# Decode attention on one core: w1 as the moving operand, and the last columns of the last K and V through transfers with an outermost dimension of three

## The chip, the cores and the metric

One core of a Trainium2 chip. The time is the device time of one execution in microseconds. In the profiles PE is the engine for matrix products (PEld its loading of weights), DVE the one for vectors, ACT for functions of single values, POOL is GpSimd, and SP only issues transfers here. Of the DMA queues, q1 carries the kernel's data (572.54 MB in before), q8 and q14 its instructions (40 packets and 14; the page calls both "instruction"). The landings and single packets given below (times of a semaphore's increments, lengths of packets) were read from the packed traces; the profile's views don't list them.

## The reference, cut to what matters

A gated mix of a one-token attention block (32 heads, a cache of 16384 positions of 128, batch 2) and an MLP block. The cache is 537 MB, the weights are 36 MB.

```python
def _A_ref(x, k_cache, v_cache, wq, wo):
    q = (x @ wq).reshape(B, Sq, H, Dh).transpose(0, 2, 1, 3)
    scores = jnp.einsum("bhqd,bhkd->bhqk", q, k_cache) * (Dh ** -0.5)
    p = softmax(scores, axis=-1)
    o = jnp.einsum("bhqk,bhkd->bhqd", p, v_cache)
    return o.transpose(0, 2, 1, 3).reshape(B, Sq, H * Dh) @ wo
# _B_ref: h = gelu(layernorm(x) @ w1) goes through shifts along the sequence;
# with one position every shift gives zeros, so x1 = x + 0 @ w2
# x1 + gelu(layernorm(x1) @ w3) @ w4;   result: g * a + (1 - g) * b
```

Softmax does not care in which order the positions stand, as long as K and V have the same order within a head.

## The kernel before

Two heads make one tile: 128 partitions, each with 256 consecutive positions (columns) of 128 bf16, 64 KB a partition. Three such buffers go round. All loads are issued on one queue (SP); `w4` and `wo` come last, `wo` in pieces that get smaller.

```python
    V_SPLIT_LAST = [NJ // 2, NJ // 2]          # NJ = 256
    def cache_rows(cache, i):
        b, hg = tiles[i]
        return cache[b, hg * G : (hg + 1) * G].rearrange("a s d -> (a s) d").rearrange(
            "(p j) d -> p j d", p=P)
    def load_k(i):
        t = big_tile("Kn")
        nc.sync.dma_start(
            out=t[:].rearrange("p (j d) -> p j d", d=Dh), in_=cache_rows(A_k_cache, i))
        kn_tiles[i] = t
    # ... load_v: the same, the last V in two pieces of 128 columns
    W4_SPLIT = [7] * 4
    WO_SPLIT = [4] * 6 + [2, 2, 1, 1, 1, 1]
    # ...
    def st_mix():                              # once, after the fifth V tile
        layernorm(xT[:], xn1T[:])
        h1 = const.tile([P, KC, B], FP32, name="h1")
        nc.vector.tensor_copy(out=h1[:], in_=linear("w1", xn1T)[:])   # w1 stationary: 64 matmuls
        gelu(h1[:], hT[:], KC)
        # ... x1 = xT + linear("w2", zeros); layernorm(x1); start_out
```

Of the kernel before, what the change touches and what calls it, by code (L numbers as in the profile page):

```python
# [10 lines left out]
FP32 = mybir.dt.float32  # L11
BF16 = mybir.dt.bfloat16
ACTF = mybir.ActivationFunctionType
ALU = mybir.AluOpType
# [9 lines left out]
def kernel(  # L24
# [15 lines left out]
    nc = tc.nc  # L40
    P = nc.NUM_PARTITIONS
    B, Sq, D = A_x.shape
    _, H, Sk, Dh = A_k_cache.shape
    F = B_w3.shape[1]
    assert Sq == 1 and Dh == P and B == 2 and H == 32
    G = 2
    NJ = G * Sk // P
# [4 lines left out]
    KC = D // P  # L52
    FC = F // P
    scale = float(Dh) ** -0.5
    NHG = H // G
    NT = B * NHG
# [5 lines left out]
    const = ctx.enter_context(tc.tile_pool(name="const", bufs=1))  # L62
# [8 lines left out]
    def misc_psum(shape, dtype=FP32):  # L71
        return mps.tile(shape, dtype, tag="misc", name="misc")

    def big_tile(name):
        return big.tile([P, SLOT], BF16, tag="big", name=name)

    def t_tile(shape, dtype, name="T"):
        return tpool.tile(shape, dtype, tag="T", name=name)
# [4 lines left out]
    kn_tiles = {}  # L83
    vn_tiles = {}
    wt = {}
    V_SPLIT_LAST = [NJ // 2, NJ // 2]

    def cache_rows(cache, i):
        b, hg = tiles[i]
        return cache[b, hg * G : (hg + 1) * G].rearrange("a s d -> (a s) d").rearrange(  # L90
            "(p j) d -> p j d", p=P
        )

    def load_k(i):
        t = big_tile("Kn")
        nc.sync.dma_start(
            out=t[:].rearrange("p (j d) -> p j d", d=Dh), in_=cache_rows(A_k_cache, i)
        )
        kn_tiles[i] = t

    def load_v(i):
        t = big_tile("Vn")
        tv = t[:].rearrange("p (j d) -> p j d", d=Dh)
        src = cache_rows(A_v_cache, i)
        j0 = 0
        for n in V_SPLIT_LAST if i == NT - 1 else [NJ]:
            nc.sync.dma_start(out=tv[:, j0 : j0 + n, :], in_=src[:, j0 : j0 + n, :])
            j0 += n
        vn_tiles[i] = t

    def load_rows(keys, srcs):

# [26 lines left out]
    def load_first():  # L139
# [12 lines left out]
        out=perm[:].rearrange("k (h a) -> k h a", a=4),  # L152
        in_=ident_f[:].rearrange("k (a h) -> k h a", a=4),
# [26 lines left out]
    for g in range(1, 4):  # L180
        nc.vector.tensor_tensor(
            out=osel_f, in0=osel_f, in1=ident_f[:, 40 * g : 40 * g + 8], op=ALU.add
# [9 lines left out]
        out=pick[:], in_=ident_f[:].rearrange("p (g w) -> p g w", w=32)[:, :, 0:B]  # L192
# [28 lines left out]
    omg_bc = const.tile([P, B], FP32)  # L221
# [21 lines left out]
    def group(g):  # L243
        return slice(32 * g, 32 * g + B)

    def zero_rows(ps, g, width):
        nc.tensor.matmul(
            ps[32 * g : 32 * g + 32, :],
            lhsT=perm[:, 0:32],
            rhs=zero[:].to_broadcast([P, width]),  # L250
            start=True,
            stop=False,
            skip_group_check=True,
        )
# [180 lines left out]
    def start_out(x1):  # L435
        for g in range(NQ):
            zero_rows(out_acc, g, QW)
        res = const.tile([P, KC, B], FP32, name="cen")
        nc.vector.tensor_tensor(out=res[:], in0=x1, in1=over_r(omg_bc[:]), op=ALU.mult)
        for c in range(KC):  # L440
            for g in range(NQ):
                nc.tensor.matmul(
                    out_acc[group(g), c:QW:KC],
                    lhsT=res[:, c, :],
                    rhs=ident_f[:, 32 * g : 32 * g + 32],
                    start=False,
                    stop=False,
                    skip_group_check=True,
                )
# [16 lines left out]
    def layernorm(src, dst):  # L466
        part = stat.tile([P, B], FP32, name="part")
        nc.vector.reduce_sum(out=part[:], in_=src.rearrange("p r b -> p b r"), axis=AX.X)
        mean = stat.tile([P, B], FP32, name="mean")
        nc.vector.tensor_scalar(  # L470
            out=mean[:], in0=total(part[:])[:], scalar1=1.0 / D, scalar2=None, op0=ALU.mult
        )
        cen = const.tile([P, KC, B], FP32, name="cen")
        nc.vector.tensor_tensor(out=cen[:], in0=src, in1=over_r(mean[:]), op=ALU.subtract)
        sq = const.tile([P, KC, B], FP32, name="cen_sq")
        nc.vector.tensor_tensor(out=sq[:], in0=cen[:], in1=cen[:], op=ALU.mult)
        part2 = stat.tile([P, B], FP32, name="part")
        nc.vector.reduce_sum(out=part2[:], in_=sq[:].rearrange("p r b -> p b r"), axis=AX.X)
        ve = stat.tile([P, B], FP32, name="mean")
        nc.vector.tensor_scalar(  # L480
            out=ve[:], in0=total(part2[:])[:], scalar1=1.0 / D, scalar2=LN_EPS, op0=ALU.mult, op1=ALU.add
        )
        rstd = stat.tile([P, B], FP32, name="rstd")
        nc.gpsimd.tensor_tensor(
            out=rstd[:], in0=ve[:], in1=neg_half[:].to_broadcast([P, B]), op=ALU.pow
        )
        nc.vector.tensor_tensor(out=dst, in0=cen[:], in1=over_r(rstd[:]), op=ALU.mult)

    def gelu(pre_f32, dst_bf, C, weight=None):
        sq = t_tile([P, C, B], FP32, "gelu")  # L490
        nc.vector.tensor_tensor(out=sq[:], in0=pre_f32, in1=pre_f32, op=ALU.mult)
        nc.vector.tensor_scalar(
            out=sq[:], in0=sq[:], scalar1=GELU_C1, scalar2=1.0, op0=ALU.mult, op1=ALU.add
        )
        nc.vector.tensor_tensor(out=sq[:], in0=sq[:], in1=pre_f32, op=ALU.mult)
        nc.scalar.activation(out=sq[:], in_=sq[:], func=ACTF.Tanh, scale=GELU_C0)
        nc.vector.tensor_scalar(
            out=sq[:], in0=sq[:], scalar1=1.0, scalar2=0.5, op0=ALU.add, op1=ALU.mult
        )
        if weight is not None:  # L500
            nc.vector.tensor_tensor(
                out=sq[:], in0=sq[:], in1=weight.unsqueeze(1).to_broadcast([P, C, B]), op=ALU.mult
            )
        nc.vector.tensor_tensor(out=dst_bf, in0=sq[:], in1=pre_f32, op=ALU.mult)

    def linear(key, actT):

        w = wt.pop(key)
        R, C = w.shape[1], w.shape[2] // P
        ps = misc_psum([P, C, B])  # L510
        for c in range(C):
            for r in range(R):
                nc.tensor.matmul(  # L513
                    ps[:, c, :],
                    lhsT=w[:, r, :].rearrange("k (p c) -> k p c", c=C)[:, :, c],
                    rhs=actT[:, r, :],
                    start=(r == 0),
                    stop=(r == R - 1),
                )
        return ps  # L520

    xn1T = const.tile([P, KC, B], BF16)
    hT = const.tile([P, KC, B], BF16)
    shT = const.tile([P, KC, B], BF16)
    x1 = const.tile([P, KC, B], FP32)
    xn2T = const.tile([P, KC, B], BF16)
    h2T = const.tile([P, FC, B], BF16)

    def st_mix():
        layernorm(xT[:], xn1T[:])  # L530
        h1 = const.tile([P, KC, B], FP32, name="h1")
        nc.vector.tensor_copy(out=h1[:], in_=linear("w1", xn1T)[:])
        gelu(h1[:], hT[:], KC)
        nc.vector.memset(shT[:], 0.0)
        for s in range(Sq):
            for blk, shift in enumerate((1, -1, 2, -2)):
                if 0 <= s - shift < Sq:
                    raise NotImplementedError("one position only")
        nc.vector.tensor_tensor(out=x1[:], in0=xT[:], in1=linear("w2", shT)[:], op=ALU.add)
        layernorm(x1[:], xn2T[:])  # L540
        start_out(x1[:])

    def st_up():
        h2 = t_tile([P, FC, B], FP32, "h2")
        nc.vector.tensor_copy(out=h2[:], in_=linear("w3", xn2T)[:])
        gelu(h2[:], h2T[:], FC, omg_bc[:])

    def st_down():
        w4 = wt.pop("w4")
# [4 lines left out]

    extra = {
        NT // 8: (lambda: load_rows(["w1", "w2"], [B_w1, B_w2]), st_mix),
        NT // 4: (lambda: load_rows(["w3"], [B_w3]), st_up),
    }
    xfers = [("big", "q", load_first)]
# [41 lines left out]
    rows = t_tile([P, QW], BF16, "rows")  # L601
    nc.vector.tensor_copy(out=rows[:], in_=out_acc[:])  # L602
    for b, queue in enumerate((nc.sync, nc.scalar)):
        queue.dma_start(
            out=out[b].rearrange("s (g n) -> (s g) n", g=NQ), in_=rows[b : 96 + b + 1 : 32, :]
# [31 lines left out]
```

## Time and profile before

| | before |
|---|---|
| time, median of 3 (later of 6) | 1337.64 us (1337.59) |
| bytes read, rate | 572.5 MB, 429 GB/s |
| DMA queue q1, share of 16 engines | 99.2% |
| PE, DVE busy | 60%, 57% |

The page of the kernel before; the row "GB/s" has 40 slices of the span, and the last rows are the DMA queues.

```profile
span 1335.9 us, 11948 instructions
PE 795.9 (60%) x5000; PEld 355.3 (27%) x5063; DVE 757.1 (57%) x998; ACT 26.8 (2%) x68; POOL 12.9 (1%) x40
DMA  9999999999999999999999999999999999999997
GB/s 409 436 438 434 421 438 428 437 438 432 428 435 435 439 424 434 430 436 438 438 427 432 430 432 438 436 432 432 432 436 438 427 430 432 438 436 438 424 423 302
q1 hardware_dynamic: 12664, 572.54, 99.2%
q8 instruction: 40, 0.66, 0.2%
q14 instruction: 14, 0.11, 0.0%
```

The transfers bound the kernel in every slice but the last. That last slice is not full, and it says why the mean over 16 engines is not enough: some engines end early. The trace shows it directly. A transfer of these completes in 16 increments of a semaphore, read here as one from each of the 16 engines. This is the first half of the last V, the 16 times in order (us from the span's start):

```
1275.97 1276.03 1276.22 1276.48 1276.59 1276.64 1276.91                    seven early engines
1281.73 1281.83 1281.84 1283.24 1283.27 1283.35 1283.40 1283.51            eight in the middle
1285.70                                                                   one straggler
```

For the first K the 16 lie within 1.7 us. A transfer has landed when its slowest engine has (the last increment of the last K comes at 1256.74 us, DVE starts on it at 1256.77), so the straggler alone sets the end: the last piece of `wo` completes at 1332.18 us on it, at 1329.93 on the next one. It falls back by about 0.97 us each time a packet of 8 KB of one series on q14 comes, mostly every 116.8 us: at these times the distance from the earliest engine to it grows in one step (8.89 to 9.86 us after the packet at 1202 us).

Two stretches of 6 us while the last K and the last V are on their way: busy time of the engines, granted clock, share of DMA time, and the rate in the last column.

```profile
core 0: us, PE busy (x) PEld busy (x) DVE busy (x) ACT busy (x) POOL busy (x), PEclk, DMA share, GB/s
1246.00:1252.00 6.00, 0.73 (x4) 0.50 (x2) 1.65 (x6) 0.78 (x2) 0.00 (x0) 0.51 1.01 437
1288.00:1294.00 6.00, 4.13 (x34) 1.90 (x35) 0.17 (x2) 0.00 (x0) 0.00 (x0) 0.50 0.96 412
```

Lines of the timeline of before: the first transposes after the w1 stage, those of the last K, the wait for the last V, and the end.

```profile
266.16 2.37 DVE L325 STREAM_TRANSPOSE T<-Kn 128x1024 f32<-128x1024 f32 x2 [5.29 <-DMA Kn<-in_A_k_cache_dram]
...
1256.77 2.37 DVE L325 STREAM_TRANSPOSE T<-Kn 128x1024 f32<-128x1024 f32 x2 [7.19 <-DMA Kn<-in_A_k_cache_dram]
...
1295.41 3.64 PE L377 MATMUL O<-Vn,PT 128*32 128x512 bf16 x32 [3.14 <-DMA Vn<-in_A_v_cache_dram]
...
1332.22 0.39 PE L426 MATMUL out_acc<-wo,Q 128*2 128x256 bf16 x4 [0.25 <-DMA wo<-in_A_wo_dram]
1332.66 0.42 DVE L602 CAST rows<-out_acc 128x256 bf16<-128x256 f32 x1 [29.59 <-PE out_acc L426]
1333.11 1.36 ACTq L604 DMA_DIRECT2D out_dram<-rows  x1
```

The bracket is the idle time before, and what ended it: each of these waits, except that of the last copy for PE, is for a transfer, and after the last piece of `wo` only some 3.7 us are left.

### The profile page before, as it was taken

To read this page: it belongs to the slowest core of one execution; us is meant where nothing else is said; L and a number is where in the kernel's file an instruction comes from. 1 tells how busy PE (TensorE), PEld (TensorE's weight loads), DVE (VectorE), ACT (ScalarE), POOL (GpSimd) and SP (SyncE) were. 2 spreads that over 40 slices of the span, in tenths; PEclk is the share of its full clock that TensorE was granted. 3 is DMA by queue.
4 is the path that set the end of the run, shared out by engine and by line. 5 is a ranking of instruction groups with operands and counts; after the bars stand their busy time and mean duration, and the time that the engine had idled before them with its cause. 6 is when DMAs were issued, how large, how long until landed. Compare 5 with 4: busy or idle time off the path is not lost.

```text
span 1335.9 us, 11948 instructions
## 1 busy us (share of the span) xinstructions
PE 795.9 (60%) x5000; PEld 355.3 (27%) x5063; DVE 757.1 (57%) x998; ACT 26.8 (2%) x68; POOL 12.9 (1%) x40
## 2 busy tenths in 40 slices
PE   2576655676656665555666555566655556665564
PEld 0223222432225222222222222232222222222232
DVE  1677665366652665555666555566655556665540
ACT  0000000000000000000000000000000000000000
POOL 0000000000000000000000000000000000000000
PEclk9788777688776877778887777888777788877775
DMA  9999999999999999999999999999999999999997
GB/s 409 436 438 434 421 438 428 437 438 432 428 435 435 439 424 434 430 436 438 438 427 432 430 432 438 436 432 432 432 436 438 427 430 432 438 436 438 424 423 302
DMA packets 12726, 573.31 MB, mean 429 GB/s; under 512 B 1784, under 2 KB 1792, under 8 KB 2560
## 3 DMA queue, kind: packets, MB, share of 16 engines
q1 hardware_dynamic: 12664, 572.54, 99.2%
q8 instruction: 40, 0.66, 0.2%
q14 instruction: 14, 0.11, 0.0%
q10 hardware_dynamic: 8, 0.00, 0.0%
HBM read 572.53 MB, written 0.00 MB: 429 GB/s over the span
## 4 chain that ended last, share of the span: by engine, by line
PE 26%; DVE 25%; DMA 23%; another core or an unknown queue 12%; issue 11%; ACT 1%; SPq 0%; ACTq 0%; POOL 0%
DVE T L325 19%; PE S L333 15%; DMA Kn<-in_A_k_cache_dram 13%; PE O L377 7%; DMA wt<-in_B_w_dram 4%; DMA Vn<-in_A_v_cache_dram 3%; DMA wo<-in_A_wo_dram 3%; PE misc L212 2%; DVE Os L392 2%; PE misc L513 2%; ACT Pr L361 1%; DVE PT L365 1%; DVE mx L354 1%; PE misc L400 1%
## 5 line engine op out<-in xcount | busy, mean ns | idle before, releaser
L333 PE MATMUL S<-T,z 128*128 128x512 bf16 x1985 | 582.1, 421 | 334.3 <-DVE T L325 312.2
L325 DVE STREAM_TRANSPOSE T<-Kn 128x1024 f32<-128x1024 f32 x512 | 612.5, 1230 | 261.2 <-DMA Kn<-in_A_k_cache_dram 209.6
L333 PEld LDWEIGHTS <-z 128*128 128x128 bf16 x2048 | 210.8, 104 | 692.3 <-issue 529.8
L377 PE MATMUL O<-Vn,PT 128*32 128x512 bf16 x2048 | 121.4, 390 | 3.1 <-DMA Vn<-in_A_v_cache_dram 3.1
L377 PEld LDWEIGHTS <-PT 128*32 128x32 bf16 x2048 | 74.2, 141 | 49.2 <-issue 20.3
L388 DVE TENSOR_SCALAR Os<-O,xmask 128x128 f32<-128x128 f32 x32 | 11.2, 350 | 101.2 <-PE O L377 101.2
L212 PE MATMUL misc<-rs,ones_f 128*128 128x2 f32 x64 | 17.9, 349 | 79.1 <-DVE rs L408 79.1
L361 ACT ACTIVATE Pr<-S,nb 128x512 bf16<-128x512 f32 x32 | 22.0, 687 | 1203.4 <-DVE nb L356 1165.8
L344 DVE TENSOR_REDUCE m<-S 128x1 f32<-128x512 f32 x32 | 22.1, 692 | 36.9 <-PE S L333 36.9
L400 PE MATMUL misc<-asel,Os 128*128 128x2 f32 x64 | 12.4, 264 | 51.0 <-DVE Os L392 51.0
L365 DVE STREAM_TRANSPOSE PT<-Pr 128x512 bf16<-128x512 bf16 x32 | 22.7, 711 | 28.7 <-ACT Pr L361 28.7
L212 PEld LDWEIGHTS misc<-rs,ones_f 128*128 128x128 f32 x64 | 16.1, 312 | 84.0 <-issue 81.2
L392 DVE SCALAR_TENSOR_TENSOR Os<-O,xmask,Os 128x128 f32<-128x128 f32 x96 | 33.7, 351 | 3.4
L400 PEld LDWEIGHTS misc<-asel,Os 128*128 128x128 f32 x64 | 9.7, 191 | 65.2 <-DVE Os L392 60.9
L212 PE MATMUL misc<-mdiag,ones_f 128*128 128x128 f32 x64 | 15.5, 325 | 17.1 <-DVE mdiag L347 17.1
L354 DVE TENSOR_REDUCE mx<-misc 64x1 f32<-64x64 f32 x64 | 14.2, 222 | 19.1 <-PE misc L212 18.6
L513 PEld LDWEIGHTS <-wt 128*128 128x128 bf16 x352 | 22.3, 172 | 9.7 <-DMA wt<-in_B_w_dram 8.4
L301 POOL TENSOR_TENSOR z<-qsel,own 128x32 bf16<-128x32 bf16 x32 | 10.8, 338 | 1207.3 <-PE S L333 1177.4
L513 PE MATMUL misc<-xn2T,wt 128*128 128x2 bf16 x224 | 14.4, 202 | 8.2 <-DMA wt<-in_B_w_dram 8.2
L412 DVE RECIPROCAL rinv<-misc 128x2 f32<-128x2 f32 x32 | 5.5, 170 | 22.6 <-PE misc L212 22.6
L269 PE MATMUL misc<-wt,xT 128*2 128x512 bf16 x64 | 5.8, 540 | 19.7 <-DVE xT L257 19.7
L602 DVE CAST rows<-out_acc 128x256 bf16<-128x256 f32 x1 | 0.4, 423 | 29.6 <-PE out_acc L426 29.6
(82 smaller groups left out, 104.6 us busy)
## 6 DMA issues: line engine op xcount, KB each, us to landing
Vn<-in_A_v_cache_dram SPq DMA_DIRECT2D x2, 4096.0 KB, 47.1
wt<-in_B_w_dram SPq DMA_DIRECT2D x1, 7168.0 KB
w<-in_B_w_dram SPq DMA_DIRECT2D x4, 1792.0 KB, 31.4
wo<-in_A_wo_dram SPq DMA_DIRECT2D x6, 1024.0 KB, 33.2
wt<-in_B_w_dram SPq DMA_DIRECT2D x2, 2048.0 KB, 37.3
wo<-in_A_wo_dram SPq DMA_DIRECT2D x2, 512.0 KB, 18.7
wo<-in_A_wo_dram SPq DMA_DIRECT2D x4, 256.0 KB, 12.7
Kn<-in_A_k_cache_dram SPq DMA_DIRECT2D x32, 52.3
```

The lines of the kernel that those rows point to most:

```text
L212: nc.tensor.matmul(ps[:], lhsT=ones_f[:], rhs=src, start=True, stop=True)
L325: nc.vector.transpose(out=T[:].rearrange("p w j s -> p j w s"), in_=Kw[:, m * CW : (m + 1) * CW].rearrange("p (j w e) -> p j w e", w=2, e=32),
L333: nc.tensor.matmul(S[:], lhsT=z[:, v, NM - 1 - m : NM - 1 - m + P], rhs=Tb[:, v // 2, :, v % 2], start=(m == 0 and v == 0), stop=(m == NM ...
L344: nc.vector.reduce_max(out=m[:], in_=S[:], axis=AX.X)
L354: nc.vector.reduce_max(out=mx[pa, :], in_=mall[pa, pa], axis=AX.X)
L361: nc.scalar.activation(out=Pr[:], in_=S[:], func=ACTF.Exp, bias=nb[:], scale=scale, accum_out=rs[:])
L365: nc.vector.transpose(out=PT[:], in_=Pr[:])
L377: nc.tensor.matmul(O[32 * g : 32 * g + 32, :], lhsT=PT[:, m : CJ * 32 : 16], rhs=V[:, j0 : j0 + 4, :], start=(m == 0), stop=(m == NM - 1),)
L388: nc.vector.tensor_scalar(out=Os[:], in0=Ox, scalar1=xmask[:, 0:1], scalar2=None, op0=ALU.mult)
L392: nc.vector.scalar_tensor_tensor(out=Os[:], in0=Ox, scalar=xmask[:, x : x + 1], in1=Os[:], op0=ALU.mult, op1=ALU.add,)
L400: nc.tensor.matmul(oc[:], lhsT=Os[:], rhs=asel[:], start=True, stop=True)
L513: nc.tensor.matmul(ps[:, c, :], lhsT=w[:, r, :].rearrange("k (p c) -> k p c", c=C)[:, :, c], rhs=actT[:, r, :], start=(r == 0), stop=(r == ...
```

## The change

Its intent, as far as the code shows it: `w1` streams through the PE as the moving operand (18 matmuls of 512 columns in place of 64 weight loads with 2 columns each). And 7 of the 256 columns of the last K and V are taken from the 16-engine transfers and loaded by transfers whose source has an outermost dimension of three, so that few engines carry them and the others have less to do. The order of rows changes, in K and V alike.

```diff
+    NARROW = 7
+    def load_cache(cache, i, name, pieces):
+        # ... t, tv, src as before
+        wide = NJ - NARROW if i == NT - 1 else NJ
+        for n in range(pieces):
+            j = slice(wide * n // pieces, wide * (n + 1) // pieces)
+            nc.sync.dma_start(out=tv[:, j, :], in_=src[:, j, :])
+        if wide < NJ:
+            half, ways = P // G, 3
+            for p0 in range(0, P, half):
+                rows = slice(p0, p0 + half // ways * ways)          # 63 rows
+                nc.sync.dma_start(
+                    out=tv[rows, wide:NJ, :],
+                    in_=src[rows, wide:NJ, :].rearrange("(y x) j d -> x y (j d)", x=ways))
+            rest = slice(half - 1, P, half)                         # rows 63 and 127
+            nc.sync.dma_start(out=tv[rest, wide:NJ, :], in_=src[rest, wide:NJ, :])
     def st_mix():
         layernorm(xT[:], xn1T[:])
-        nc.vector.tensor_copy(out=h1[:], in_=linear("w1", xn1T)[:])
-        gelu(h1[:], hT[:], KC)
+        # ... ps zeroed in two groups
+        for r in range(KC):
+            for g in range(2):
+                nc.tensor.matmul(ps[group(g), :], lhsT=xn1T[:, r, :],
+                                 rhs=w1[:, r, g * HW : (g + 1) * HW], ...)
+        nc.vector.tensor_copy(out=h1[0:64, :], in_=ps[0:64, :])
+        gelu(h1[0:64, :], h_rows[0:64, :])
```

More of the change, by code (lines that the diff above doesn't have):

```diff
@@ L85 @@
     wt = {}
-    V_SPLIT_LAST = [NJ // 2, NJ // 2]
+    NARROW = 7
     def cache_rows(cache, i):
@@ L92, in cache_rows @@
         )
-    def load_k(i):
-        t = big_tile("Kn")
-        nc.sync.dma_start(
-            out=t[:].rearrange("p (j d) -> p j d", d=Dh), in_=cache_rows(A_k_cache, i)
-        )
-        kn_tiles[i] = t
-    def load_v(i):
-        t = big_tile("Vn")
-        tv = t[:].rearrange("p (j d) -> p j d", d=Dh)
-        src = cache_rows(A_v_cache, i)
-        j0 = 0
-        for n in V_SPLIT_LAST if i == NT - 1 else [NJ]:
-            nc.sync.dma_start(out=tv[:, j0 : j0 + n, :], in_=src[:, j0 : j0 + n, :])
-            j0 += n
-        vn_tiles[i] = t
+    def load_cache(cache, i, name, pieces):
+        t = big_tile(name)
+        tv = t[:].rearrange("p (j d) -> p j d", d=Dh)
+        src = cache_rows(cache, i)
+        wide = NJ - NARROW if i == NT - 1 else NJ
[8 more added lines that the diff above has]
+                    out=tv[rows, wide:NJ, :],
+                    in_=src[rows, wide:NJ, :].rearrange("(y x) j d -> x y (j d)", x=ways),
+                )
+            rest = slice(half - 1, P, half)
+            nc.sync.dma_start(out=tv[rest, wide:NJ, :], in_=src[rest, wide:NJ, :])
+        return t
+    def load_k(i):
+        kn_tiles[i] = load_cache(A_k_cache, i, "Kn", 1)
+    def load_v(i):
+        vn_tiles[i] = load_cache(A_v_cache, i, "Vn", 2 if i == NT - 1 else 1)
     def load_rows(keys, srcs):
@@ L487, in layernorm, with gelu @@
         nc.vector.tensor_tensor(out=dst, in0=cen[:], in1=over_r(rstd[:]), op=ALU.mult)
-    def gelu(pre_f32, dst_bf, C, weight=None):
-        sq = t_tile([P, C, B], FP32, "gelu")
+    def gelu(pre_f32, dst_bf, weight=None):
+        shape = list(pre_f32.shape)
+        sq = t_tile(shape, FP32, "gelu")
         nc.vector.tensor_tensor(out=sq[:], in0=pre_f32, in1=pre_f32, op=ALU.mult)
@@ L501, in gelu @@
             nc.vector.tensor_tensor(
-                out=sq[:], in0=sq[:], in1=weight.unsqueeze(1).to_broadcast([P, C, B]), op=ALU.mult
+                out=sq[:], in0=sq[:], in1=weight.unsqueeze(1).to_broadcast(shape), op=ALU.mult
             )
@@ L522 @@
     xn1T = const.tile([P, KC, B], BF16)
-    hT = const.tile([P, KC, B], BF16)
+    h_rows = const.tile([P, D // 2], BF16)
     shT = const.tile([P, KC, B], BF16)
@@ L530, in st_mix @@
         layernorm(xT[:], xn1T[:])
-        h1 = const.tile([P, KC, B], FP32, name="h1")
-        nc.vector.tensor_copy(out=h1[:], in_=linear("w1", xn1T)[:])
-        gelu(h1[:], hT[:], KC)
+        w1 = wt.pop("w1")
+        HW = D // 2
+        ps = misc_psum([P, HW])
+        for g in range(2):
+            zero_rows(ps, g, HW)
+        for r in range(KC):
+            for g in range(2):
+                nc.tensor.matmul(
+                    ps[group(g), :],
+                    lhsT=xn1T[:, r, :],
+                    rhs=w1[:, r, g * HW : (g + 1) * HW],
+                    start=False,
+                    stop=(r == KC - 1),
+                    skip_group_check=True,
+                )
+        h1 = t_tile([P, HW], FP32, "h1")
+        nc.vector.tensor_copy(out=h1[0:64, :], in_=ps[0:64, :])
+        gelu(h1[0:64, :], h_rows[0:64, :])
         nc.vector.memset(shT[:], 0.0)
@@ L545, in st_up @@
         nc.vector.tensor_copy(out=h2[:], in_=linear("w3", xn2T)[:])
-        gelu(h2[:], h2T[:], FC, omg_bc[:])
+        gelu(h2[:], h2T[:], omg_bc[:])
     def st_down():
```

## The prediction

> **What bounds the kernel now.** The DMA queue, from start to end. The page shows DMA busy 99.2% of 16 engines' span, 572.5 MB at 429 GB/s; PE is busy 60%, DVE 57%. K and V tiles land every 19.3 us. But the 16 engines are not equally late. Of the 16 completions that the trace keeps per transfer, those of the first K spread over 1.7 us, of the last over 9.8 us. At the first half of the last V: seven engines complete at 1276.0 to 1276.9, eight at 1281.7 to 1283.5, one alone at 1285.7. That one falls back by about 0.97 us every 116.8 us, when an 8 KB instruction packet of q14 appears; the eight share the 40 packets (16 KB) of q8. This straggler sets the end: the last wo piece lands at 1332.18 on it, at 1329.93 on the next one. Then about 3.7 us follow (4 matmuls, a 0.42 us copy, the output): span 1335.9, time 1337.64.
>
> **What the change does.**
> 1. Last K and V: 7 of 256 columns leave the 16-engine transfer. A 64 KB packet takes 2.418 us and an engine has 8 per tile, so every engine is relieved of 7/256 x 19.34 = 0.53 us per tensor, 1.06 us for both. The columns come back in transfers of 63 rows with an outermost dimension of three. [...] Each of them gets 42 rows of 1792 B per tensor; a 2048 B packet takes 84 ns and starts every 80, so about 70 ns each: 2.9 us per tensor, 5.9 us for both, net +4.8 us.
> 2. w1 as moving operand: 64 weight loads and matmuls become 18 of 512 columns, 3.9 us against about 3; gelu runs on 64x512 instead of 128x16, six DVE operations of about 0.6 us instead of 0.17, so about 3 us longer on DVE. The timeline shows DVE idle 5.29 us after this stage until the next K lands. Off the critical path: 0.
>
> **Critical share.** Only item 1 counts. If engines 0 to 2 are among the seven early ones (9.7 us ahead of the straggler), they absorb 4.8 us and the straggler's relief of 1.06 us comes out whole: 1337.64 - 1.06 = 1336.6. The trace has no engine numbers, so this is inferred from the design. If one of the three is of the eight middle ones, the end moves by about +2.5 us (1340); if it is the straggler, by +4.8 us.
>
> **Predicted: 1336.6 us**, range 1335.9 to 1339.6. Faster by over 2%: 0.005; within 2%: 0.985; slower: 0.01.
>
> **What would show it.** Right: last wo landing near 1331.1, spread of the last completions about 1 us less between straggler and first group, three engines some 5 us later than the other four early ones after the last V; gelu on DVE longer, the following transposes unmoved.
>
> **What would make it wrong.** One engine taking all 63 rows (+8 us); small packets far slower than 80 ns; engines 0 to 2 not early; a changed instruction count moving the fetch packets to or from the straggler (1 us each); the eight completion semaphores, now shared with six small transfers, delaying the issue of w4 or wo until an engine starves.

1337.64, less 1.06 for the relief of the straggler, 0 for w1, is 1336.6 us. The author took the narrow transfers to run on three engines. "Each of them" means each of these three, "engines 0 to 2" here and in the expectations; no trace numbers the engines. Two of the prediction's readings, looked up in the trace of before: the engines in the middle fall back one by one with the packets of q8 (4 engines lie over 1.1 us behind the earliest in the tile that completes from 138.44 us on; in the tiles after the packets at 155.44, 188.99 and 225.26 us it is 5, 6 and 7), and the completions of all transfers come on eight semaphores.

## The result

| | before | after |
|---|---|---|
| median of 6 runs | 1337.59 us | 1339.76 us |
| range | 1337.41 to 1337.76 | 1339.55 to 1339.89 |
| ratio, 95% interval | | 1.0016 (1.0003 to 1.0029) |

Ratios here are the mean time of one kernel's fast runs over that of the other's of the same rounds, so not quite the ratio of the medians. The change costs 2.2 us (0.16%) where 1.0 us of gain was predicted.

The page of the kernel after, the same lines:

```profile
span 1338.0 us, 11864 instructions
PE 796.8 (60%) x4954; PEld 353.4 (26%) x5017; DVE 758.7 (57%) x998; ACT 27.2 (2%) x68; POOL 13.3 (1%) x40
GB/s 408 437 435 437 434 422 439 428 434 439 435 429 429 436 435 439 435 426 430 430 436 438 437 436 433 430 428 435 440 430 433 432 432 437 435 438 430 406 404 311
q1 hardware_dynamic: 12936, 572.54, 99.3%
q8 instruction: 39, 0.64, 0.2%
```

The bytes are the same. Two slices near the end have fallen, from 424 and 423 to 406 and 404 GB/s. The same stretches while the last K and V are on their way:

```profile
core 0: us, PE busy (x) PEld busy (x) DVE busy (x) ACT busy (x) POOL busy (x), PEclk, DMA share, GB/s
1246.00:1252.00 6.00, 0.89 (x4) 0.64 (x4) 1.65 (x6) 0.78 (x2) 0.00 (x0) 0.61 1.01 328
1288.00:1294.00 6.00, 4.12 (x33) 1.76 (x34) 0.99 (x3) 0.18 (x2) 0.00 (x0) 0.52 0.99 316
```

The DMA engines are no less busy than before (1.01 and 0.99) and move about a quarter less: 328 for 437 GB/s, 316 for 412. A packet only lasts longer. The timeline of after, and the new transfers among its DMA issues (count, KB each):

```profile
265.92 2.37 DVE L336 STREAM_TRANSPOSE T<-Kn 128x1024 f32<-128x1024 f32 x2 [4.71 <-DMA Kn<-in_A_k_cache_dram]
...
1257.74 1.25 DVE L336 STREAM_TRANSPOSE T<-Kn 128x1024 f32<-128x1024 f32 x1 [8.00 <-DMA Kn<-in_A_k_cache_dram]
...
1297.42 3.21 PE L388 MATMUL O<-Vn,PT 128*32 128x512 bf16 x27 [4.11 <-DMA Vn<-in_A_v_cache_dram]
...
1334.12 0.39 PE L437 MATMUL out_acc<-wo,Q 128*2 128x256 bf16 x4 [0.24 <-DMA wo<-in_A_wo_dram]
1334.55 0.42 DVE L629 CAST rows<-out_acc 128x256 bf16<-128x256 f32 x1 [30.14 <-PE out_acc L437]
1335.01 1.43 ACTq L631 DMA_DIRECT2D out_dram<-rows  x1
```

```profile
Kn<-in_A_k_cache_dram SPq DMA_DIRECT2D x1, 7968.0 KB
...
Kn<-in_A_k_cache_dram SPq DMA_DIRECT2D x2, 110.2 KB
```

The last K arrives 1.0 us later than before although its transfer is shorter, the last V 2.0 us, and the end is 1.9 us later. The 16 completions of the first half of the last V (124 columns now, 128 before):

```
1276.59 1276.69 1277.15 1277.17                                            four early engines
1279.67 1280.07 1280.20                                                    three that were early
1282.21 1282.28 1282.48 1282.51 1283.95 1283.96 1283.99 1284.15            eight in the middle
1286.37                                                                    the straggler
```

So the three engines were early ones and took the extra work without being last; that step of the prediction was right. But the straggler, which by these times is none of the three, is late too (1286.37 us for 1285.70). In the trace the packets of the other 13 engines are stretched while the 1792 B packets run: those of 63744 B, 2.352 us at their usual, last up to 3.73 us. All stretches added are 21 us for K, which is 1.6 us for each of the 13 engines.

### The profile page after: what moved, and what is told of

Its sections match the earlier page's. It is cut to its first block, busy times and chain, and to the rows that moved or that the text cites. A ratio compares the mean times of both kernels' runs of the same rounds, so it can differ in the third digit from the quotient of the medians.

```text
span 1338.0 us, 11864 instructions
## 1 busy us (share of the span) xinstructions
PE 796.8 (60%) x4954; PEld 353.4 (26%) x5017; DVE 758.7 (57%) x998; ACT 27.2 (2%) x68; POOL 13.3 (1%) x40
## 4 chain that ended last, share of the span: by engine, by line
DVE 25%; PE 24%; DMA 23%; issue 14%; another core or an unknown queue 12%; ACT 1%; SPq 0%; ACTq 0%; POOL 0%
DVE T L336 19%; DMA Kn<-in_A_k_cache_dram 13%; PE S L344 13%; PE O L388 7%; DMA wt<-in_B_w_dram 4%; DMA Vn<-in_A_v_cache_dram 3%; DMA wo<-in_A_wo_dram 3%; PE misc L223 2%; DVE Os L403 2%; PE misc L525 1%; ACT Pr L372 1%; DVE PT L376 1%; DVE mx L365 1%; PE misc L411 1%
## 5 line engine op out<-in xcount | busy, mean ns | idle before, releaser
L525 PEld LDWEIGHTS <-wt 128*128 128x128 bf16 x288 | 18.2, 164 | 8.8 <-DMA wt<-in_B_w_dram 7.9
```

The lines of the kernel that those rows point to most:

```text
L525: nc.tensor.matmul(ps[:, c, :], lhsT=w[:, r, :].rearrange("k (p c) -> k p c", c=C)[:, :, c], rhs=actT[:, r, :], start=(r == 0), stop=(r == ...
```

## The experiments

Times are medians; "before" was run beside each of them and stayed at 1337.42 to 1337.49 us.

Three theories of the hold-up were at hand. **Port**: the three engines write into partitions to which other engines are writing at the same time, and that holds engines up. Three sets of 24 partitions are tried below: for 0 to 11 and 32 to 43 the theory expected no hold-up, for the two others one. The ground for that choice was an assumption that no run shows (the packets in the traces carry neither an engine nor a partition). "These three engines" in foreign_345 are three that the theory expected to be held up there. **HBM**: their rows lie 64 KB apart in HBM, and short reads so far apart hold up every engine. **Few engines or short packets** as such.

### The two halves of the change apart

w1_only:

```diff
-        wide = NJ - NARROW if i == NT - 1 else NJ
+        wide = NJ
```

> The w1 half of the change without the narrow transfers. All theories: 1337.4 to 1337.7 us, the same as before within 0.3 us, because this stage sits in idle time of DVE and PE. If it is near 1338.5 or more, the w1 half carries part of the 2.2 us and the transfer theories are too large by that.

Measured: 1337.46 us (1337.24 to 1337.57), ratio 1.0000.

narrow_only is before with the new loading functions and the old st_mix and gelu.

> The narrow transfers without the w1 half. All theories: the whole 2.2 us, 1339.6 to 1340.0 us, and in the trace the other 13 engines' packets stretched (63744 B packets from 2.35 us to over 3 us) while the 1792 B packets run. The two halves together should add up to the change's 2.2 us.

Measured: 1339.78 us (1339.59 to 1339.90), ratio 1.0017. The narrow transfers carry all of it, the w1 half nothing. In the timeline of after, the idle time of DVE ahead of the next K shrank from 5.29 to 4.71 us; the w1 half is absorbed there.

### What about the narrow transfers is slow

narrow16:

```diff
-            for p0 in range(0, P, half): ...      # transfers on three engines
-            nc.sync.dma_start(out=tv[rest, wide:NJ, :], in_=src[rest, wide:NJ, :])
+            nc.sync.dma_start(out=tv[:, wide:NJ, :], in_=src[:, wide:NJ, :])
```

> The same 7 columns, the same 1792 B rows 64 KB apart in HBM, as one ordinary transfer of 128 rows that all 16 engines share[...]. Port theory (three engines write into partitions that the other engines are writing to[...]): no stretching, 1337.4 to 1337.8 us. HBM theory[...]: still stretched, 1339 us or more. Theory of short packets as such: also 1339 us or more.

Measured: 1337.61 us (1337.49 to 1337.81), ratio 1.0001; every 1792 B packet took 74 ns. Same bytes, same short rows 64 KB apart, no hold-up. The stretch of the last K:

```profile
1246.00:1252.00 6.00, 1.00 (x4) 0.75 (x4) 1.65 (x6) 0.78 (x2) 0.00 (x0) 0.59 1.04 449
```

contig_src (a wrong result):

```diff
-                    in_=src[rows, wide:NJ, :].rearrange("(y x) j d -> x y (j d)", x=ways),
+                    in_=flat[p0 * NJ : p0 * NJ + half // ways * ways * NARROW, :].rearrange(
+                        "(y x j) d -> x y (j d)", x=ways, j=NARROW),
```

> The same three-engine transfers into the same partitions, but read from one contiguous stretch of HBM (wrong data on purpose, so a wrong result). HBM theory: no stretching, the predicted relief comes out, 1336.3 to 1336.9 us. Port theory: unchanged against the change, 1339.5 to 1340.0 us, packets of the other engines still above 3 us.

Measured: 1339.80 us (1339.45 to 1340.07), ratio 1.0018, and the rate fell just as in the change:

```profile
1246.00:1252.00 6.00, 0.86 (x4) 0.62 (x4) 1.65 (x6) 0.78 (x2) 0.00 (x0) 0.60 1.00 328
```

The HBM theory falls with these two: where the rows are read from makes no difference. Short packets as such fall with narrow16. Port and few engines are left.

### Which partitions are written

These four start from w1_only and add, ahead of `w4`, transfers into the unused 8 KB at the end of w4's buffer, so that only the destination differs. Their results are right; the bytes are never read.

```diff
+        if key == "w4":
+            spare = whole[:, sum(split) * D :]
+            src = cache_rows(A_v_cache, NT - 1)
+            for n, p0 in enumerate((0, 32)):       # own_ports; (12, 44): foreign_345; (64, 96): foreign_8910
+                nc.sync.dma_start(
+                    out=spare[p0 : p0 + 12, : 4 * 896].rearrange("p (n e) -> p n e", e=896),
+                    in_=src[64 * n : 64 * n + 48, NJ - 7 : NJ, :].rearrange(
+                        "(x y n) j d -> x y n (j d)", x=3, n=4))
+    # spread_extra: the change's own two transfers of 63 rows, into spare[rows, 0:896]
```

> The w1 half alone (1337.46 us) plus, ahead of w4, two extra three-engine transfers of 48 rows of 1792 B each, read 64 KB apart, into unused space at the end of w4's buffer: partitions 0 to 11 and 32 to 43[...]. Port theory: no packet of another engine is stretched, engines 0 to 2 finish about 2.3 us later (32 rows at 70 ns each) and they have that much to spare: 1337.3 to 1337.8 us. Rival (any transfer on three engines, or short packets on three engines, holds up all 16): stretched 14336 B and 32768 B packets, 1338.5 us or more.

Measured: 1339.99 us (1339.73 to 1340.52), which looked like the end of the port theory. It was not the experiment that was meant. In the trace of after a narrow transfer of 63 rows, issued at 1203.80 us, shows 4 updates of its semaphore: 1 at 1205.08 us and 3 as it lands (1248.62, 1249.29 and 1249.34 us); the transfer of two rows shows 1 and 2. This is read as 1 at once and then 1 from each engine that the transfer uses, so 3 engines and 2. own_ports' transfers show 13, so 12 engines: "(x y)" was presumably merged to one dimension. So it shows the hold-up on 12 engines (368 GB/s between 1284 and 1290 us, where w1_only has 414), and rules out that three engines are what it takes.

> As own_ports, with the same source and size, into partitions 12 to 23 and 44 to 55[...]. Port theory: only these three engines (and engines 0 to 2, which wait for them) are held up, by 2.1 us or more[...], the other ten not at all; the time rises only if one of the three is the straggler or of the middle group. Rival (something shared by all engines): all 13 are held up alike.

Measured: 1340.70 us (1340.23 to 1341.33). 

> As foreign_345, into partitions 64 to 75 and 96 to 107[...]. Port theory: three other engines are held up than in foreign_345, by the same amount; together the two runs tell which group the straggler is in. Rival: no difference from foreign_345.

Measured: 1339.88 us (1339.77 to 1340.03). Both use the pattern of own_ports, 12 engines by its count, and tell no more than it.

> As own_ports, but the two extra transfers are those of the change: 63 rows each over all partitions, 126 rows of 1792 B. All theories that fit the change: every engine is held up once by about 1.6 us (what the change's two tensors showed each), 1338.8 to 1339.3 us. It is the control for the other three: same place in the program, only the partitions differ.

Measured: 1341.78 us, but its four runs lie from 1339.16 to 1342.79, and only the lowest is where it was expected. In the profiled run the hold-up is there between 1286 and 1290 us; after it, for some 35 us, the packets lasted about a tenth longer (those of 14336 B 0.596 us for 0.535; 383 GB/s between 1308 and 1320 us, 426 in w1_only). No other run shows that, and its cause stays open. As a control the run is spoilt.

The next three use longer rows in a pattern that was not merged: they ran on three engines (4 updates in the trace).

```diff
-                    out=spare[p0 : p0 + 12, : 4 * 896]..., in_=...
+                    out=spare[p0 : p0 + 12, : 28 * Dh],
+                    in_=src[64 * n : 64 * n + 12, NJ - 28 : NJ, :].rearrange(
+                        "(y x) j d -> x y (j d)", x=3),
```

> The run own_ports did not test what it was meant to: its completions (12 engine completions, not 3) show that the access pattern was merged and the transfers ran on 12 engines[...]. Here the pattern can't be merged: two transfers of 12 rows of 7168 B ahead of w4, on three engines, into partitions 0 to 11 and 32 to 43[...]. Port theory (writing into partitions that another engine is writing to): no packet of another engine is stretched; engines 0 to 2 are about 2.1 us later (57 KB each at the engine's 27 GB/s), which they have to spare; 1337.2 to 1337.8 us. Rival (a transfer on few engines holds up all): stretched packets on the other 13 engines, 1338.5 us or more.

> As own_three into partitions 12 to 23 and 44 to 55[...]. Port theory, narrow form: exactly three further engines are held up, by 2.1 us or more; the other ten see no stretched packet. Port theory, wide form[...]: all 13 are stretched. Time 1337.3 us to 1340.5 us, depending on whether the straggler is one of the three.

> As foreign_three_345 into partitions 64 to 75 and 96 to 107[...]. Narrow form: three other engines are held up than in foreign_three_345. Wide form: all alike.

| run | time, us | ratio | other engines' packets |
|---|---|---|---|
| own_three | 1337.66 (1337.61 to 1337.73) | 1.0001 | none stretched but one, by 0.55 us, as happens in before too; 7168 B packets 272 ns |
| foreign_three_345 | 1339.95 (1339.67 to 1340.33) | 1.0019 | stretched by 27 us in all; 7168 B packets up to 562 ns |
| foreign_three_8910 | 1339.63 (1339.54 to 1339.72) | 1.0016 | stretched by 28 us in all; 7168 B packets up to 576 ns |

The same transfers, three engines each time, the same source, 57 KB an engine; only the partitions differ. The rate between 1284 and 1290 us, first of w1_only, which has no such transfers, then of own_three, of foreign_three_345 and of foreign_three_8910:

```profile
1284.00:1290.00 6.00, 2.86 (x25) 1.66 (x28) 2.18 (x9) 0.78 (x2) 0.00 (x0) 0.61 0.96 414
```

```profile
1284.00:1290.00 6.00, 2.82 (x22) 1.80 (x26) 2.19 (x9) 0.78 (x2) 0.00 (x0) 0.75 0.96 411
```

```profile
1284.00:1290.00 6.00, 2.85 (x25) 1.63 (x28) 2.19 (x9) 0.78 (x2) 0.00 (x0) 0.71 1.03 298
```

```profile
1284.00:1290.00 6.00, 2.85 (x22) 1.80 (x26) 2.19 (x9) 0.78 (x2) 0.00 (x0) 0.80 1.02 294
```

Into partitions 0 to 11 and 32 to 43: nothing happens (411 GB/s, 414 in w1_only). Into 12 to 23 and 44 to 55, or 64 to 75 and 96 to 107: the rate falls by over a quarter (298 and 294 GB/s). And not only three engines are held up, as the narrow form of the port theory had it, but all 13 by 2.1 us each (27 or 28 us over 13), the straggler among them, with both sets of partitions. Of the two forms the wide one holds in these two runs: every engine paid. The theory named the harmless set before the runs. Why it is harmless for these three engines, when own_ports' 12 held up the others with the same set, and why the hold-up reaches all 13, is not shown by any run. In these two it cost each engine as much as the bytes of one of the three take alone (57 KB at the 65536 B in 2.418 us of an undisturbed packet: 2.1 us). That is no rule: in the change one engine's 42 rows of 1792 B, 2.8 us at that rate, cost the others 1.6 us.

narrow14:

```diff
-    NARROW = 7
+    NARROW = 14
```

> The change with 14 columns in place of 7: twice the bytes in as many rows (3584 B each). If the hold-up goes with the bytes that cross, each tensor's wide transfer loses 3.3 us in place of 1.64 and gains 1.06 by being shorter: the straggler's last K lands 2 x 1.1 us late, time 1341 to 1343 us. If it goes with the number of rows, 1.64 us a tensor against a relief of 1.06 us: 1338.4 to 1338.9 us, unless engines 0 to 2 now end last.

Measured: 1345.30 us (1345.12 to 1345.47), ratio 1.0059. The last K was 22.00 us behind the V ahead of it on the straggler; 242 of 256 columns at 19.30 us a tile would be 18.24, so the hold-up is 3.8 us, over twice that of 7 columns. It goes with the bytes, not with the rows. The end is later than expected because three other engines now end last (first piece of w4: three complete at 1306.35 to 1306.97 us, the next latest at 1304.63; by their time they are the three that carry the narrow transfers).

### Was the other term real, and what is the straggler

relief_only (a wrong result: the 7 columns are zero):

```diff
-            for p0 in range(0, P, half): ...      # all narrow transfers
+            nc.gpsimd.memset(tv[:, wide:NJ, :], 0.0)
```

> The change with the three-engine transfers taken out: the wide transfers end at column 249, the last 7 columns are set to zero by GpSimd (a wrong result on purpose). If the relief was sized rightly, every engine including the straggler ends 1.06 us earlier: 1336.3 to 1336.6 us against the w1 half's 1337.46, and the change's 1339.76 is then this plus the hold-up of 2 x 1.63 us = 3.26 us. If the relief is not real (something else sets the end), 1337.4 us.

Measured: 1336.35 us (1336.30 to 1336.40), ratio 0.9991 (0.9979 to 1.0004). The interval holds 1, but all five runs lie below all nine of before (1337.30 to 1337.90). The relief is real and of the size that was predicted. Completions of the straggler, from the traces, in us:

| | before | w1_only | relief_only | after |
|---|---|---|---|---|
| V ahead of the last K | 1237.44 | 1237.33 | 1237.16 | 1237.23 |
| last K, wide part | 1256.74 | 1256.63 | 1255.92 | 1257.72 |
| last V, wide part | 1295.37 | 1295.27 | 1294.03 | 1297.38 |
| last wo | 1332.18 | 1332.07 | 1330.84 | 1334.08 |
| first to third row | 57.93 | 57.94 | 56.87 | 60.15 |
| third to fourth row | 36.81 | 36.80 | 36.81 | 36.70 |

All of the difference arises between the first and the third row: 1.07 us less by the relief (57.94 to 56.87), then 3.28 us more by the narrow transfers (56.87 to 60.15), in sum the 2.2 us of the change.

fewer_dve (a right result), from w1_only, four small DVE instructions a tile moved to ACT:

```diff
-        nc.vector.tensor_scalar(out=mdiag[:], in0=ident_f[:], scalar1=m[:, 0:1], ...)
+        nc.scalar.activation(out=mdiag[:], in_=ident_f[:], func=ACTF.Copy, scale=m[:, 0:1])
-        nc.vector.tensor_scalar(out=nb[:], in0=mx[:], scalar1=-scale, scalar2=kill[:, 0:1], ...)
+        nc.scalar.activation(out=nb[:], in_=mx[:], func=ACTF.Identity, scale=-scale, bias=kill[:, 0:1])
-        # rs2 = hmask * rs and the first of four Os steps, on nc.vector
+        # the same two on nc.scalar with func=ACTF.Copy and a scale of one value a partition
```

> The w1 half alone, with four small DVE instructions of each K and V pair (the scaling of mdiag, nb, rs2 and the first of the four Os steps) given to ACT, which is 2% busy; all transfers as before. Theory of the straggler (it loses 0.97 us with each 8 KB packet of q14, and these bring DVE's instructions): about a tenth fewer of these packets, spaced 127 us or so in place of 116.8, the straggler ends 0 or 1 us earlier, 1336.4 to 1337.4 us, faster than both kernels if a packet falls away. If the packets are not DVE's, their spacing stays at 116.8 us and the time at 1337.4 us or, through the longer chain after each K, above.

Measured: 1336.41 us (1336.25 to 1336.70), ratio 0.9992 (0.9978 to 1.0005). Here too the interval holds 1, but all five runs lie below the same nine of before. Its page:

```profile
span 1334.7 us, 11856 instructions
PE 798.9 (60%) x4954; PEld 353.4 (26%) x5017; DVE 731.4 (55%) x870; ACT 70.7 (5%) x196; POOL 13.2 (1%) x40
```

The straggler stands at 1236.28 us at the V ahead of the last K, 1.05 us earlier than in w1_only, one packet's worth. A series of q14 packets, at 163.2 and then up to 1194.0 us in 8 steps of 129 us on average (119 to 146), replaces the one of 116.8 us, and the straggler falls back at these times. In all q14 has as many packets as before, perhaps because ACT has more instructions now (196 for 68). The packets carry no engine's name in the trace, so that they are DVE's instructions is inferred from this spacing. It is the one version here that computes the reference and beats both kernels, before by 1.0 us and the change by 3.3.

## Why the prediction was wrong, point by point

- **What bounds the kernel** (the slowest of 16 DMA engines): right. In the four kernels of the table above the end moved with the straggler's completions alone; in narrow14, where the narrow transfers carry twice the bytes, three other engines end last.
- **The w1 half: 0.** Right: 1337.46 us alone. The 16 matmuls took 3.58 us in the trace of after (predicted: about 3), the DVE operations 0.41 to 0.69 us.
- **Three engines, among the early ones**: right. The narrow transfers show 3 completions, and three of the seven early engines fell back. Which numbers they have is not shown: the traces have no engine numbers.
- **Relief of 1.06 us**: right, 1.07 us in relief_only.
- **The step that failed**: "they absorb 4.8 us and the straggler's relief of 1.06 us comes out whole". The work of the three was taken as private to them, because the engines were counted as 16 separate pipes. While their 1792 B packets run, the 13 others slow down: 1.6 us each for K, 3.28 us for K and V together on the straggler. That it comes from the partitions to which they write is inferred from own_three and the two foreign_three runs. 1337.6 - 1.1 + 3.3 = 1339.8, which is what was measured (1339.76). The term was not mis-sized; it was missing. The prediction had named about 1340 us for another case, a carrying engine that is one of the eight in the middle; that the measured time lies near it is chance, since the three that carry were early ones.
- The list of what could go wrong named small packets "far slower than 80 ns". They were slower (102 ns on average, 74 at first), but as a part of the same hold-up: in narrow16 they took 74 ns throughout.

## What to carry to other kernels

When the slowest DMA engine sets the end, look at the single completions of a transfer, not at the mean busy share. Shifting bytes to engines that are early gave 1.07 us here and cost 3.28, because the transfers that carried them held up all the others. In the runs with three engines and the same source, the partitions written decided it: writing to 0 to 11 and 32 to 43 cost nothing (own_three, 1337.66 us), to either of two other sets 2.1 us an engine. The harmless set is not so in itself: written by 12 engines it cost as much as the others (own_ports, 1339.99 us). Where the rows are read from in HBM made no difference (contig_src, 1339.80 us). And no run here shifts work without a hold-up and gains. A DMA share of 1.0 with fewer GB/s was the sign of this hold-up (1.01 and 328 GB/s for 437), though not of it alone (spread_extra shows it for 35 us more without a known cause), and the count of semaphore updates told on how many engines a transfer really ran (4 for three, 13 for 12, 16 for all).
